# Long convolution with a gate: the large stores of a_u issued by GpSimd, positions in four loads, a sixth tile for x and v

## The chip, the cores and the metric

The kernel runs on one core of a Trainium2 chip. The metric is the time of one execution on the device in microseconds (us), lower is better: 1128.43 us as the median of three runs (1128.22 to 1131.92). The engines are named as in the profile: PE (matmuls), DVE and ACT (elementwise and copies), POOL (GpSimd), SP (which here only issues DMAs). DMAs can be issued by SP, ACT and POOL.

## What is computed

For x and v of shape (4, 12800, 128):

```
h = (relu(pos_emb @ w1) @ w2) * exp(-0.01 * t)        # a filter as long as the sequence
y = irfft(rfft(x * v) * rfft(h))[:12800]              # causal long convolution per channel
a = x * y
gate = sigmoid(sum_k conv_w[k] * shift(a, 4 - k))     # 5 taps
out = (gate * (a @ w_val)) @ w_out
```

Everything is float32. The transforms of length 25600 are done as matmuls with tables, split into 2 x 100 x 64 points.

## The kernel before

The work has three stages, each with its own tile pools. Stage 1 (lines 237 to 394) multiplies x by v, does the first short transform over 100 points, and writes the spectra to a DRAM scratch tensor `a_u` (52 MB). It also makes the filter's spectra. Stage 2 (lines 397 to 525) reads `a_u` back, does the 64-point transforms, multiplies by the filter and writes `c_y` to DRAM. Stage 3 reads `c_y`, finishes the inverse, gates and projects.

The change touches stage 1 alone. It is a loop over n = 0 to 63 (line 368), with its instructions in the order in which they are written (`manual_schedule`); each engine executes its own in that order. Step n does this:

- `fetch(n + 7)`: SP issues the load of 1 MB of x and v (line 311) into one of the `XB` = 5 tiles of `held`, used in turn.
- `product(n + 3)`: DVE multiplies x by v (line 317). An even one goes to a tile `u` of its own; an odd one goes back into the loaded tile, so that this tile is held until `mirrored` has read it.
- `mirrored(q + 1)`, every second step: DVE makes sums and differences of two products in one of two `eo` tiles (lines 325, 326).
- `spectra(q, s)`: PE does 12 matmuls into two PSUM tiles (line 338), and ACT copies each to the tile `st`, of which there are four (line 340).
- some pieces of `filt()`, paced by the count of steps: first 16 pieces that read the positions (line 257), then 32 that transform them (lines 275 to 278), then 25 with the twiddles `fk` (lines 286 to 300).
- `store(q, s, st)`: the 100 rows of `st`, 8 KB each, go to `a_u` as two DMAs. ACT issues rows 0 to 95 (768 KB), POOL rows 96 to 99 (32 KB), both on line 345.
- in the first steps POOL also issues the loads of the tables (line 388).

The positions come in 16 loads of 200 KB, issued by SP (line 250) between the fetches into one tile with room for five of them, the sixth of the `ld` pool; `load_pos` is called after each of the first pieces of `filt`, and a load waits until the matmuls that read its place are done.

Every DMA signals its landing on a semaphore. Those issued by SP and by ACT share eight, in the order of the program, and those issued by POOL have eight others. A DMA waits, on the queue of the engine that issues it, until the one before it on its semaphore has landed. In the middle of the loop fetches and stores alternate on the eight, so that a fetch waits for the fetch four before it; at the end, where no fetch is left, the eight no longer alternate, and the store of step 57 has the semaphore of the last fetch.

At n = 60 SP issues the first loads of stage 2 into the same `ld` pool (line 384), and after the loop the rest of them (line 394), which wait for the last stores (line 218). Stage 2 starts when they have landed.

Of the kernel before, what the change touches and what calls it, by code (L numbers as in the profile page):

```python
# [23 lines left out]
B, S, D, FO, KC = 4, 12800, 128, 64, 5  # L24
J, N1, N2 = 2, 100, 64
M = N1 * N2
KG = 8
# [52 lines left out]
def _raw(pool, tables, src, name):  # L80
    raw = pool.tile(list(src.shape), mybir.dt.int64, name=name)
    tables.append((raw, src))
    return raw
# [46 lines left out]
def tile_longconv_gate(  # L130
# [20 lines left out]
    nc = tc.nc  # L151
# [16 lines left out]
    w1bd = const.tile([128, 128], F32, name="w1bd")  # L168
# [18 lines left out]
    def load():  # L187
        return ld.tile([128, 2048], F32, name="ld")

    ag_pool = ctx.enter_context(tc.tile_pool(name="ag", bufs=1))  # L190
    ag = ag_pool.tile([128, N1, J, FO], F32, name="ag")
# [45 lines left out]
    with tc.tile_pool(name="p1", bufs=1) as p1, tc.tile_pool(name="ps1", bufs=1, space=PSUM) as ps1:  # L237
        g_sb = p1.tile([N1, J, FO, N2], F32, name="g_sb")

        GN, E, XB = 8, 4, 5  # L240
        held = [load() for _ in range(XB + 1)]
        PE1 = GN // 2 * N1
        pos_held = held.pop()[:, 0:2048 // PE1 * PE1].rearrange("p (i q a) -> p i q a", q=GN // 2, a=N1)
        parts, pos_ts = [(c0, j) for c0 in range(0, N2, GN) for j in range(J)], []

        def load_pos():
            if len(pos_ts) < len(parts):
                c0, j = parts[len(pos_ts)]
                t = pos_held[:, len(pos_ts) % (2048 // PE1)]
                nc.sync.dma_start(out=t.rearrange("p q a -> p (q a)"), in_=pos[j, c0 // GN])  # L250
                pos_ts.append(t)

        def filt():
            for i, (n0, j) in enumerate(parts):
                gp = ps1.tile([N1, GN, FO], F32, name="gp", bufs=2)
                for q in range(GN // 2):
                    nc.tensor.matmul(
                        out=gp[:, 2 * q:2 * q + 2].rearrange("a n e -> a (n e)"),
                        lhsT=pos_ts[i][:, q], rhs=w1bd, start=True, stop=True)
                nc.vector.scalar_tensor_tensor(  # L260
                    g_sb[:, j, :, n0:n0 + GN], gp.rearrange("a n e -> a e n"), 0.0,
                    win[:, j, n0:n0 + GN].unsqueeze(1).to_broadcast([N1, FO, GN]),
                    op0=ALU.max, op1=ALU.mult)
                load_pos()
                yield 1.5

            for j in range(J):
                for e0 in range(0, FO, E):
                    ap = ps1.tile([128, E, N1], F32, name="ap", bufs=2)
                    for e in range(E):  # L270
                        terms = [(j, 0, 1)] if j == 0 else [(1, 0, 1), (0, 1, 2)]
                        for i, (jj, wr, wi) in enumerate(terms):
                            lhs = g_sb[:, jj, e0 + e]
                            fl = dict(start=(i == 0), stop=(i == len(terms) - 1))
                            nc.tensor.matmul(out=ap[0:N2, e], lhsT=lhs, rhs=fwd[:, wr], **fl)
                            nc.tensor.matmul(out=ap[N2:2 * N2, e], lhsT=lhs, rhs=fwd[:, wi], **fl)
                    nc.scalar.copy(
                        out=ag[:, :, j, e0:e0 + E].rearrange("p k e -> p e k"), in_=ap)
                    yield 1.0 + 0.7 * j

            after = None
            for k0 in range(0, N1, 4):
                fk = p1.tile([128, 4, 2 * N2], F32, name="fk", bufs=2)
                for i in range(4):
                    k1 = k0 + i
                    nc.scalar.activation(fk[:, i], dft[:, 1], AF.Copy, scale=tw[:, 1, k1:k1 + 1])
                for i in range(4):
                    k1 = k0 + i
                    nc.vector.scalar_tensor_tensor(
                        fk[:, i], dft[:, 0], tw[:, 0, k1:k1 + 1], fk[:, i], op0=ALU.mult, op1=ALU.add)  # L290
                if after:
                    after()

                def after(k0=k0, fk=fk):
                    gz = ps1.tile([128, 4, 2 * N2], F32, name="gp", bufs=2)
                    for i in range(4):
                        nc.tensor.matmul(
                            out=gz[:, i], lhsT=ag[:, k0 + i].rearrange("p j e -> p (j e)"), rhs=fk[:, i],
                            start=True, stop=True)
                    nc.scalar.copy(out=ag[:, k0:k0 + 4].rearrange("p k j e -> p k (j e)"), in_=gz)  # L300
                yield 1.9
            after()
            yield 0.5
# [5 lines left out]
        def fetch(i):  # L309
            t = held[i % XB]  # L310
            nc.sync.dma_start(out=t, in_=xv[n_seq[i]].rearrange("h q w j l b d -> (h q) (w j l b d)"))
            fetched[i] = t.rearrange("p (w e) -> p w e", w=2)

        def product(i):
            t = fetched.pop(i)
            u = p1.tile([128, J * 2 * XE], F32, name="u", bufs=1) if i % 2 == 0 else t[:, 0]
            nc.vector.tensor_tensor(u, t[:, 0], t[:, 1], op=ALU.mult)
            us[i] = u

        def mirrored(q):  # L320

            a, b = us.pop(2 * q), us.pop(2 * q + 1)
            eo = held_e[q % 2]
            for s, op in ((0, ALU.add), (1, ALU.subtract)):
                nc.vector.tensor_tensor(eo[:, s].rearrange("p j l e -> p (j l e)"), a, b, op=op)  # L325
                nc.vector.tensor_tensor(eo[:, s, :, 0], eo[:, s, :, 0], eo[:, s, :, 1], op=ALU.subtract)
            eos[q] = eo
# [13 lines left out]
            return st  # L341

        def store(q, s, st):
            for eng, r in ((nc.scalar, slice(0, 96)), (nc.gpsimd, slice(96, N1))):
                eng.dma_start(  # L345
                    out=a_u[r, s, q].rearrange("k e j b d -> k (e j b d)"),
                    in_=st[r].rearrange("k e j b d -> k (e j b d)"))

        fetched, us, eos = {}, {}, {}
        with tc.manual_schedule():  # L350
            held_e = [p1.tile([128, 2, J, 2, XE], F32, name=f"eo{i}") for i in range(2)]
            fetch(0)
            raws = [
                (dst, _raw(p1, tables, src, f"raw{i}"))
                for i, (dst, src) in enumerate(((wval, w_val), (wout, w_out), (cw, conv_w.rearrange("k d -> d k"))))]
            fil = filt()
            narrow = (None for dst, raw in raws for _ in _narrow(nc, p1, dst, raw))
            n_fil, spent = 16 * 1.5 + 16 * 1.0 + 16 * 1.7 + 25 * 1.9 + 0.5, 0.0
            for i in range(1, XB):
                fetch(i)  # L360
                load_pos()
            product(0)
            product(1)
            mirrored(0)
            product(2)
            for i in (XB, XB + 1):
                fetch(i)
            for n in range(N2):
                q, s = divmod(n, 2)
                if n + XB + 2 < N2:  # L370
                    fetch(n + XB + 2)
                if n + 3 < N2:
                    product(n + 3)
                if s == 0 and q + 1 < N2 // 2:
                    mirrored(q + 1)
                st = spectra(q, s)
                while spent < n_fil * (n + 1) / (N2 - 6):
                    step = next(fil, None)
                    if step is None:
                        break  # L380
                    spent += step
                if n == N2 - 4:
                    for p in range(2):
                        loaded[p] = load_pair(p, NL)
                store(q, s, st)
                if n and tables:
                    dst, src = tables.pop(0)
                    nc.gpsimd.dma_start(out=dst, in_=src)
                if n >= 14:
                    next(narrow, None)  # L390
            for _ in fil:
                pass
            for p in range(2):
                load_a(loaded[p][0], p, NL, N2 // 2)


    with tc.tile_pool(name="p2", bufs=1) as p2, tc.tile_pool(name="psz", bufs=1, space=PSUM) as psz, \
# [62 lines left out]
        with tc.manual_schedule():  # L460
            for p in range(-1, NP + 1):
# [8 lines left out]
                if p == 41:  # L470
                    j, g = y_order[0]
                    nc.sync.dma_start(
                        out=xr_first, in_=xt[j][:, g * R:(g + 1) * R].rearrange("d n b a -> d (n b a)"))
# [23 lines left out]
                if now:  # L497
# [6 lines left out]
                    if old:  # L504
                        held = p2.tile([128, 1], F32, name="held", bufs=2)
# [30 lines left out]
    with tc.tile_pool(name="y3", bufs=1) as y3, tc.tile_pool(name="psy", bufs=1, space=PSUM) as psy, \  # L536
# [147 lines left out]
        with tc.manual_schedule():  # L684
# [7 lines left out]
            for i in range(R * NT + AHEAD3 + R + 3):  # L692
                (s, r), (t, rt) = divmod(i, R), divmod(i - AHEAD3, R)
                if r == 0 and s < NT:
                    if s + 1 < NT:
                        load_rows(s + 1)
                    j, g = y_order[s]
# [79 lines left out]
```

## Time and profile before

| | |
|---|---|
| median of 3 runs | 1128.43 us |
| profiled execution | 1130.9 us |
| its span, first to last instruction | 1128.9 us |
| stage 1, to the first matmul of stage 2 | 341 us |
| PE, DVE, ACT, POOL busy | 92%, 87%, 55%, 62% of the span |
| DMA, mean over the span | 317 GB/s |
| chain that ended last | PE 63%, DMA 22%, DVE 11%, ACT 3% |

The profile is of one execution. A share of the DMA near 1.0 in a stretch means that all 16 DMA engines had packets in work; the GB/s beside it say how fast those packets went. "Idle before" of an instruction is the time for which its engine had nothing to do, with what ended it behind the arrow. Times in the rows are microseconds from the start of the span.

### The profile page before, as it was taken

Reading aid. Unit: us, or ns where it says so; the run is one execution under the profiler, and the core shown is the slowest. Engines: PE = TensorE matmul, PEld = TensorE weight load, DVE = VectorE, ACT = ScalarE, POOL = GpSimd, SP = SyncE. Lnnn points to the kernel's source line nnn. Section 1 sums busy time; section 2 is a strip of 40 time slices with the busy share of each in tenths; the row PEclk is TensorE's granted clock in tenths of the full one; section 3 lists DMA queues with packets and bytes.
Section 4 is the critical chain, followed back from the end, with each engine's and each line's share of the span. In section 5 each row is a group of like instructions: output and inputs, shape, how many; then the busy total and the mean of one; then the engine's idle time right before and its main releaser. Section 6 shows DMA issues by size and latency. Waiting matters only on the chain.

```text
span 1128.9 us, 17155 instructions
## 1 busy us (share of the span) xinstructions
PE 1038.0 (92%) x6204; PEld 490.9 (43%) x6204; DVE 980.8 (87%) x1214; ACT 619.1 (55%) x1003; POOL 698.1 (62%) x405
## 2 busy tenths in 40 slices
PE   5789997977868999999999999979999999999996
PEld 2345654534423444444444444434444444444442
DVE  6677657888817999999999999739999999999997
ACT  1347665866642444444344444346767777767673
POOL 1111110100016888898898889638999899999981
PEclk9899999999986999999999999998999999999999
DMA  9999999999987788888988999566888888888842
GB/s 376 414 415 410 395 380 368 391 371 372 338 263 245 257 302 310 304 298 309 315 302 288 373 339 329 163 193 262 342 318 346 305 349 314 350 313 351 314 181 116
DMA packets 87771, 357.95 MB, mean 317 GB/s; under 512 B 9269, under 2 KB 18278, under 8 KB 65073
## 3 DMA queue, kind: packets, MB, share of 16 engines
q1 hardware_dynamic: 45768, 224.74, 55.0%
q10 hardware_dynamic: 39408, 129.18, 29.3%
q0 software_dynamic: 2512, 2.94, 0.9%
q8 instruction: 50, 0.82, 0.3%
q14 instruction: 33, 0.26, 0.1%
HBM read 225.76 MB, written 131.07 MB: 316 GB/s over the span
## 4 chain that ended last, share of the span: by engine, by line
PE 63%; DMA 22%; DVE 11%; ACT 3%; issue 1%; SPq 0%; ACTq 0%; DVEq 0%
PE c_ps L442 20%; DMA ld<-in_xv_dram 17%; PE sd L601 9%; PE z_ps L426 9%; PE o_ps L664 7%; PE v_ps L654 6%; PE tp L615 5%; PE fp L338 3%; DMA ld<-in_pos_dram 3%; PE c_ps L411 2%; DVE gt L643 2%; DVE eo L325 2%; DMA c_y<-c_sb 1%; DVE va L432 1%; DVE vb L432 1%
## 5 line engine op out<-in xcount | busy, mean ns | idle before, releaser
L628 POOL TENSOR_TENSOR ext<-yr,xr 128x400 f32<-128x400 f32 x120 | 304.4, 2538 | 38.1 <-DVE yr L626 32.7
L643 DVE SCALAR_TENSOR_TENSOR gt<-ext,cw,gt 128x1600 f32<-128x1600 f32 x128 | 242.7, 1896 | 2.4 <-ACT gt L640 2.4
L338 PE MATMUL fp<-eo,fold 64*128 64x512 f32 x768 | 194.8, 643 | 35.2 <-ACT st L340 19.0
L446 ACT COPY c_sb<-c_ps 128x1024 f32<-128x1024 f32 x100 | 101.3, 1013 | 207.3 <-PE c_ps L442 207.3
L345 POOL DMA_DIRECT2D a_u<-st x64 | 33.2, 519 | 290.4 <-ACT st L340 245.2
L340 ACT COPY st<-fp 128x1024 f32<-128x1024 f32 x128 | 126.7, 1016 | 117.9 <-PE fp L338 81.7
L442 PE MATMUL c_ps<-va,ld 64*128 64x512 f32 (+1 forms) x800 | 165.7, 554 | 0.0
L432 DVE TENSOR_TENSOR va<-z_ps,h_sb 128x2048 f32<-128x2048 f32 x50 | 114.5, 2290 | 30.4 <-PE z_ps L426 30.4
L426 PE MATMUL z_ps<-ld 64*64 64x512 f32 x800 | 123.0, 619 | 9.8 <-DMA ld<-a_u 8.7
L601 PE MATMUL sd<-ag,fold 100*64 100x512 f32 (+1 forms) x512 | 127.9, 617 | 2.9 <-DMA ag<-c_y 2.9
L509 POOL TENSOR_TENSOR va<-va,vb 128x1024 f32<-128x1024 f32 x49 | 116.0, 2367 | 15.9 <-DVE vb L432 15.9
L338 PEld LDWEIGHTS fp<-eo,fold 64*128 64x128 f32 x768 | 73.4, 199 | 115.4 <-issue 59.8
L442 PEld LDWEIGHTS c_ps<-va,ld 64*128 64x128 f32 x800 | 74.1, 189 | 112.2 <-issue 111.7
L664 PE MATMUL o_ps<-gd,wout 128*128 128x400 f32 x256 | 111.5, 517 | 10.7 <-DVE gd L659 9.8
L513 POOL TENSOR_TENSOR va<-va,vb 128x1024 f32<-128x1024 f32 x50 | 119.1, 2383 | 0.0
L432 DVE TENSOR_TENSOR vb<-z_ps,h_sb 128x2048 f32<-128x2048 f32 x50 | 114.0, 2281 | 0.0
L608 ACT COPY sd_sb<-sd 128x512 f32<-128x512 f32 x128 | 76.7, 599 | 57.6 <-PE sd L601 57.0
L654 PE MATMUL v_ps<-ext,wval 128*128 128x400 f32 x256 | 107.3, 501 | 0.0
L442 PE MATMUL c_ps<-vc,ld 64*128 64x512 f32 x400 | 94.2, 589 | 0.0
L615 PEld LDWEIGHTS tp<-ident,sd_sb 128*128 128x128 f32 x512 | 58.9, 142 | 79.2 <-PE sd L601 48.7
L510 POOL TENSOR_TENSOR vc<-vc,vd 128x768 f32<-128x768 f32 x49 | 89.2, 1820 | 1.9
L615 PE MATMUL tp<-ident,sd_sb 128*128 128x128 f32 x512 | 81.0, 283 | 4.7 <-ACT sd_sb L608 3.4
(86 smaller groups left out, 1484.9 us busy)
## 6 DMA issues: line engine op xcount, KB each, us to landing
ld<-in_xv_dram SPq DMA_DIRECT2D x64, 1024.0 KB
ag<-c_y SPq DMA_DIRECT2D x58, 1024.0 KB
c_y<-c_sb ACTq DMA_DIRECT2D x100, 512.0 KB
a_u<-st ACTq DMA_DIRECT2D x64, 768.0 KB
ld<-a_u SPq DMA_DIRECT2D x48, 1024.0 KB
xr<-in_xt_dram SPq DMA_DIRECT2D x31, 800.0 KB
out_dram<-o_sb ACTq DMA_DIRECT2D x31, 800.0 KB
ld<-in_tab_w_dram SPq DMA_DIRECT2D x12, 768.0 KB
```

Source lines behind the costliest of these rows:

```text
L338: nc.tensor.matmul(out=fp[:, h], lhsT=fold[r, w], rhs=eo[r, o, :, l], start=i == 0, stop=i == len(terms) - 1)
L340: nc.scalar.copy(out=st[:, o].rearrange("k j (h b) d -> k h j (b d)", h=2), in_=fp)
L426: nc.tensor.matmul(out=zs[c][half[h]], lhsT=wk[half[c], 0, half[h]], rhs=a2[half[c], h, j], start=True, stop=True)
L432: nc.vector.tensor_tensor(out, z.rearrange("p (b d) -> p b d", d=D).unsqueeze(1).to_broadcast([128, n, B, D]), h_sb.unsqueeze(2).to_broadc ...
L442: nc.tensor.matmul(out=c_ps[:, h, 0:n], lhsT=wk[half[h], 1 + c], rhs=vt[half[h]].rearrange("p b d -> p (b d)"), start=(i == 0), stop=(i == ...
L513: nc.gpsimd.tensor_tensor(va[:, 2:4], va[:, 2:4], vb[:, 2:4], op=ALU.add)
L601: nc.tensor.matmul(out=sd[c * N2:(c + 1) * N2], lhsT=inv[k, s // NG, c], rhs=ct[c][k, r * B * D:(r + 1) * B * D], start=True, stop=True)
L615: nc.tensor.transpose(out=tp[:, b], in_=t[:, b], identity=ident)
L628: nc.gpsimd.tensor_tensor(e[:, r0 + r], yr, xr, op=ALU.mult)
L643: nc.vector.scalar_tensor_tensor(gt, rows(t, k), cw[:, k:k + 1], gt, op0=ALU.mult, op1=ALU.add)
L654: nc.tensor.matmul(out=v_ps, lhsT=wval, rhs=rows(t)[:, r * ROW:(r + 1) * ROW], start=True, stop=True)
L664: nc.tensor.matmul(out=o_ps, lhsT=wout, rhs=gd, start=True, stop=True)
```

## The change

Three things change in stage 1. POOL issues both DMAs of a store. The positions are laid out on the host so that four loads of 800 KB bring all of them, to the tile `ag`, which later takes the filter's spectra; they are issued once, behind fetches 1 to 4. And the tile that held positions is now a sixth one for x and v (`XB` = 6), so that the fetch in step n is number n + 8.

```
-        GN, E, XB = 8, 4, 5
-        held = [load() for _ in range(XB + 1)]
+        GN, E, XB = 8, 4, 6
+        held = [load() for _ in range(XB)]
...
+        pos_ts = ag.rearrange("p k j e -> p (k j e)")[:, 0:len(parts) * PE1].rearrange(
+            "p (i q a) -> p i q a", q=GN // 2, a=N1)
+
+        def load_pos(i):
+            nc.sync.dma_start(out=pos_ts[:, 4 * i:4 * i + 4].rearrange("p i q a -> p (i q a)"), in_=pos[i])
...
-                        lhsT=pos_ts[i][:, q], rhs=w1bd, start=True, stop=True)
+                        lhsT=pos_ts[:, i, q], rhs=w1bd, start=True, stop=True)
...
-                load_pos()
                 yield 1.5
...
         def store(q, s, st):
-            for eng, r in ((nc.scalar, slice(0, 96)), (nc.gpsimd, slice(96, N1))):
-                eng.dma_start(
+            for r in (slice(0, 96), slice(96, N1)):
+                nc.gpsimd.dma_start(
...
             for i in range(1, XB):
                 fetch(i)
-                load_pos()
+                if i < 5:
+                    load_pos(i - 1)
```

## Rows read from the trace of the kernel before

**Rows 1.** The page, part 2: the span in 40 slices of 28 us.
```profile
DMA  9999999999987788888988999566888888888842
GB/s 376 414 415 410 395 380 368 391 371 372 338 263 245 257 302 310 304 298 309 315 302 288 373 339 329 163 193 262 342 318 346 305 349 314 350 313 351 314 181 116
```
**Rows 2.** Stretches: length, busy us (instructions) of PE, PEld, DVE, ACT, POOL, clock, DMA, GB/s.
```profile
56.00:85.00 29.00, 25.91 (x162) 13.76 (x158) 22.77 (x25) 14.35 (x15) 5.11 (x9) 1.00 1.02 415
...
113.00:285.00 172.00, 148.76 (x1108) 83.90 (x1108) 129.96 (x209) 115.55 (x190) 17.64 (x34) 0.96 0.99 380
285.00:311.00 26.00, 21.27 (x108) 10.84 (x104) 22.42 (x34) 16.63 (x31) 2.59 (x5) 1.00 0.97 330
311.00:338.00 27.00, 17.96 (x92) 7.34 (x92) 5.06 (x5) 11.85 (x12) 3.11 (x6) 0.84 0.84 270
```
**Rows 3.** SP's waits from 64 to 345 us: in total, times, longest.
```profile
SPq L311 <- DMA ld<-in_xv_dram: 153.5, 36, 8.1
SPq L311 <- DVE eo L325: 42.7, 11, 8.6
```
**Rows 4.** ACT in order of time from 268 to 346 us: start, duration, idle before.
```profile
299.82 0.31 ACTq L345 DMA_DIRECT2D a_u<-st  x1
...
304.17 0.58 ACT L300 COPY ag<-gp 128x512 f32<-128x512 f32 x1 [0.62 <-PE gp L297]
311.35 0.31 ACTq L345 DMA_DIRECT2D a_u<-st  x1
311.78 1.93 ACT L340 COPY st<-fp 128x1024 f32<-128x1024 f32 x2 [7.03 <-DMA ld<-in_xv_dram]
...
331.30 0.31 ACTq L345 DMA_DIRECT2D a_u<-st  x1
```
**Rows 5.** DVE in order of time from 284 to 346 us.
```profile
311.30 1.23 DVE L317 TENSOR_TENSOR ld<-ld 128x1024 f32<-128x1024 f32 x1 [0.39 <-DMA ld<-in_xv_dram]
314.97 1.23 DVE L325 TENSOR_TENSOR eo<-u,ld 128x1024 f32<-128x1024 f32 x1 [2.45 <-PE fp L338]
316.24 0.69 DVE L326 TENSOR_TENSOR eo<-eo 128x512 f32<-128x512 f32 x1
```
**Rows 6.** PE in order of time, at 124 us and from 310 us.
```profile
124.48 2.85 PE L338 MATMUL fp<-eo,fold 64*128 64x512 f32 x12
128.78 1.56 PE L338 MATMUL fp<-eo,fold 64*128 64x512 f32 x6
...
312.85 8.48 PE L338 MATMUL fp<-eo,fold 64*128 64x512 f32 x24 [5.94 <-ACT st L340]
```
**Rows 7.** The chain that ended last, at the end of stage 1: start, duration.
```profile
296.46 14.81 DMA ld<-in_xv_dram
...
331.30 6.66 DMA a_u<-st
```
**Rows 8.** DMAs that POOL issues: ns least, median, most; the last row is landing.
```profile
L345 POOL DMA_DIRECT2D a_u<-st x64: 517/518/534, 19.3 to 331.6; - x64
...
DMA to landing us min/median/max: 4.8/6.7/9.2
...
L388 POOL DMA_DIRECT2D dft<-in_tab_dft_dram x1: 598/598/598, 39.6 to 39.6; - x1
```
**Rows 9.** DMA queues from 113 to 198 us: packets, MB, share of 16 engines.
```profile
q1 hardware_dynamic: 2492, 18.16, 56.4%
q10 hardware_dynamic: 1939, 13.58, 40.3%
q0 software_dynamic: 545, 0.56, 2.0%
```
**Rows 10.** SP's loads of positions: ns least, median, most, first and last start.
```profile
L250 SPq DMA_DIRECT2D ld<-in_pos_dram x16: 327/355/465, 1.7 to 61.6; - x16
```
**Rows 11.** Odd products of DVE, the first and the last of six from 113 to 169 us.
```profile
114.56 1.22 DVE L317 TENSOR_TENSOR ld<-ld 128x1024 f32<-128x1024 f32 x1 [2.60 <-DMA ld<-in_xv_dram]
...
168.20 1.23 DVE L317 TENSOR_TENSOR ld<-ld 128x1024 f32<-128x1024 f32 x1 [3.60 <-DMA ld<-in_xv_dram]
```

More of the change, by code (lines that the diff above doesn't have):

```diff
@@ L238, in tile_longconv_gate @@
         g_sb = p1.tile([N1, J, FO, N2], F32, name="g_sb")
-        GN, E, XB = 8, 4, 5
-        held = [load() for _ in range(XB + 1)]
+        GN, E, XB = 8, 4, 6
+        held = [load() for _ in range(XB)]
         PE1 = GN // 2 * N1
[L243 to L251, printed above, removed]
+        parts = [(c0, j) for c0 in range(0, N2, GN) for j in range(J)]
+        pos_ts = ag.rearrange("p k j e -> p (k j e)")[:, 0:len(parts) * PE1].rearrange(
+            "p (i q a) -> p i q a", q=GN // 2, a=N1)
+        def load_pos(i):
+            nc.sync.dma_start(out=pos_ts[:, 4 * i:4 * i + 4].rearrange("p i q a -> p (i q a)"), in_=pos[i])
         def filt():
@@ L758 @@
     pos = np.asarray(inputs["pos_emb"]).reshape(J, N1, N2 // KG, KG // 2, 2, FO)
-    pos = np.transpose(pos, (0, 2, 4, 5, 3, 1)).reshape(J, N2 // KG, 2 * FO, KG // 2 * N1)
+    pos = np.transpose(pos, (2, 0, 4, 5, 3, 1)).reshape(4, 4, 2 * FO, KG // 2 * N1)
+    pos = np.transpose(pos, (0, 2, 1, 3)).reshape(4, 2 * FO, 2 * KG * N1)
     feeds[:0] = [("xv", xv), ("xt", xt), ("pos", pos)]
```

## The prediction, made before the changed kernel was run

> **What bounds the kernel now.** I read the page's slices first, then stage 1 by stretches, then the waits of the engine that issues the loads, then the end of the stage in order of time. The slices show where to look: the DMA is full for the first eleven slices, some 310 us, and falls in the twelfth [rows 1]. That is stage 1, the only one whose code changes; stages 2 and 3 should keep their length and start when it ends. So the question is what stage 1 loses.
>
> The stretches split it in three [rows 2]. From 56 to 85 us the share is 1.02 at 415 GB/s. From 113 to 285 us it is 0.99 at 380 GB/s, from 285 to 311 us 0.97 at 330 GB/s, and from 311 to 338 us 0.84 at 270 GB/s. So the loop runs at the pace of its transfers: a step moves a load of 1,048,576 bytes and a store of 819,200, and DVE's odd product waits for a landed load each time [rows 11]. Between the two rows shown there are ten steps in 53.64 us, 5.4 us each, while PE's own round in the same place, from the start of one step's matmuls to the next, is 4.30 us [rows 6]. Compute has room, the DMA little.
>
> The waits of SP say what holds the loads: 153.5 us, in 36 waits, until an earlier load has landed, and 42.7 us until DVE has freed a tile [rows 3]. The first is the shared semaphores: only four fetches can be under way.
>
> The end of the stage is another matter. ACT copies at 304.17 us and then nothing until 311.35, where it issues a store; the copy behind it shows 7.03 us of idle time ended by a load of x and v [rows 4]. The store needed only ACT's own copies. It waited because its semaphore was that of the last fetch, and every later copy waited behind it. The last fetch lands as DVE's last product starts, 311.30 us [rows 5]. From there the last store is issued 20.0 us later, at 331.30 [rows 4], lands 6.66 us after [rows 7], and stage 2 waits for that. PE shows why it takes 20: at 312.85 it begins the steps that had piled up, the first 24 matmuls (two steps) in 8.48 us [rows 6], where two steps of the middle take 2 x 2.85 = 5.70: the granted clock of the stretch is 0.84, against 0.96 and 1.00 before [rows 2], so partly 1.2 instead of 2.4 GHz.
>
> **The change part by part.**
>
> *The stall of ACT goes.* With the stores on POOL, ACT waits for no load. What is late next is the last load itself. From its landing at 311.30 the chain is product 1.23, sums 1.23, correction 0.69 [rows 5], two steps of matmuls 2 x 2.85 [rows 6], and a last copy of 0.97 (half of the 1.93 for two, rows 4): 9.8 us, and some 0.3 between instructions. Before it was 20.0, so 9.9 less. If PE ran both steps at the speed of its 8.48 us for two, the chain is 2.8 longer, and if three steps are piled up another 2.9: 4.2 less. I take 9.9, bounds 4.2 and 10.2 (nothing between instructions).
>
> *The withheld stores compete.* Before, ACT issued no store between 299.82 and 311.35 [rows 4], and the last loads had the DMA to themselves. In the changed kernel four more stores (steps 57 to 60) come ahead of the last landing: 4 x 819,200 bytes at 380 GB/s [rows 2] are 8.6 us. Against it, the sixth tile lets SP issue the last fetch about a step sooner: it was issued at 296.46 [rows 7], and a step is 4.9 us (POOL's stores run from 19.3 to 331.6, rows 8: 63 steps in 312.3). Net 3.7 us later, bounds 0 and 8.6.
>
> *The fetches.* With loads alone on the eight semaphores, a fetch waits for the one eight before it, which six tiles never reach; the 153.5 us of waiting turn into waits for a tile or vanish. They are worth only what the DMA idles: 0.03 of 172 us and 0.05 of 26 us against the share of 1.02 [rows 2], 5.2 + 1.3 = 6.5 us. The slower packets (380 against 415 GB/s at nearly the same share) are not a matter of the queue's depth as far as the rows show. I take 2.0 of it, since the waits for a tile stay; bounds 0 and 6.5.
>
> *POOL's issues.* 64 more DMAs of 96 rows. The trace has no such one; POOL needs 0.518 us for 4 rows of 8 KB and 0.598 for 128 rows of 1 KB [rows 8], so some 0.6 us, 64 x 0.6 = 38 us on an engine that is busy 17.64 of 172 us in the middle [rows 2]. A step then costs POOL 1.1 us of 4.9. Behind a waiting store stand only its twin, the next stores, and the tables, in the first eleven steps; PE needs the first table only when the 16 position pieces are done. Cost 0, and ACT loses 64 issues of 0.31 us that nobody waited for.
>
> *Packets of the software queue.* They could be slower than ACT's. From 113 to 198 us ACT's queue used 40.3% of 16 engines for 13.58 MB, 548 us of engine time or 0.33 us per 8 KB; POOL's used 2.0% for 0.56 MB, 27 us for 68 such rows (17 stores of four) with all its small packets counted in, at most 0.40 us each [rows 9]. If all of the difference held, 64 x 96 / 16 x 0.07 = 27 us. But POOL's queue had 477 packets besides the 68 rows, and 10 ns for each of these would explain all of it: 0. They are tiny (0.56 MB is the rows alone), so I take 0; the 27 us are in the rivals.
>
> The Trainium skill's page "SBUF — State Buffer" (section "SBUF: two separate sides") warns of this very move: a DMA issued from GpSimd has its descriptors written by GpSimd, and a DVE operation in a two-port mode locks it out meanwhile; it advises issuing from ACT or SP. By that rule the two issues of the last store would each wait for a DVE instruction of up to 1.23 us, 2.5 us in all, and the sum would be -5.7. The trace does not agree for the operations used here: with DVE busy 130 of 172 us [rows 2], POOL's 64 issues took 517 to 534 ns [rows 8].
>
> *Landing.* POOL's 32 KB stores land 4.8 to 9.2 us after issue [rows 8], ACT's last one in 6.66 [rows 7]. A copy into `st` waits for the store four steps back, 4 x 4.9 = 19.6 us, less about 3 us for the copies themselves: it binds only beyond 16.6 us. Cost 0; at the last store from -2 to +2.5, the same two numbers against 6.66.
>
> *Positions.* All bytes are as before, 3.28 MB, but 4 x 614,400 of them move ahead of fetches 2 to 5: 6 us of the DMA at 415 GB/s, which delays the first steps by up to that and is given back up to 61.6 us, when the old loads ended [rows 10]. The cover is a full DMA; if steps 2 to 5 could not catch up it costs 6 us. Compute's 4.30 against the 4.9 of a step says that they can: 0. The waits of SP for the positions' place go, and no fetch stands behind them.
>
> Sum: -9.9 + 3.7 - 2.0 = -8.2 us, on the profiled execution 1130.9 - 8.2 = 1122.7. That execution lay 2.5 us over the median of 1128.43; from the median it is 1120.2, my forecast. All bounds together (with 2 less and 2.5 more for landing, 6 more for the positions) give -18.7 to +12.9: 1110 to 1141 without the 27 us.
>
> **The rivals.**
>
> *The transfers give nothing back (no change).* The DMA is the bound, and what ACT no longer loses the last loads do. For it: shares of 0.97 to 1.02 until 311 us [rows 2]. Against it: 0.84 in the last 27 us. The tail gives its lower bound of 4.2, the competing stores take 3.7, nothing else: -0.5, 1127.9. The Trainium skill's "DMA: Bandwidth & Descriptors" (section "Issuing engines are not separate DMA queues") says as much: the issuing engine saves only the time of issuing, the 16 engines are the same. By that rule the gain would be near 0; the trace agrees on the full DMA and shows at 311 us a wait that the rule does not cover.
>
> *Slower: POOL's queue is the slower one.* One mechanism, the price of a row of 8 KB in the software queue. At 0.40 us against 0.33 [rows 9] the stage grows by 27 us, less 8.2: 1147. It decides from 0.33 + 8.2 x 16 / 6144 = 0.35 us on. For it: 0.40 as the outer bound; against it, the small packets that are counted in.
>
> *Much faster.* If the four-deep queue of loads is why packets slow down after 113 us, they go at 415 again: 172 x 380 + 26 x 330 = 73.9 MB in 178 us instead of 198, 20 less, and with the tail's -9.9 + 3.7 it is 1102. Against it: nothing in the shares (0.99 and 0.97) says that engines lacked work.
>
> **How the numbers follow.** Forecast 0.54 (own range 1114 to 1126), no change 0.25, slower 0.12, much faster 0.09. A run of this kernel can tell about 0.5% from no change, 5.6 us: faster is below 1122.8, slower above 1134.1. Of the forecast 0.8 lies below 1122.8, of "no change" a quarter: faster 0.43 + 0.06 + 0.09 = 0.58; same 0.11 + 0.19 = 0.30; slower 0.12. The range 1108 to 1132 leaves out most of the slower case and half of the much faster.
>
> **What would show it.** Right: no idle time of ACT ended by a load; the last store within 10 to 13 us of the last product; the first matmul of stage 2 near 333 us instead of 341; SP waiting for DVE rather than for loads. POOL's 96-row issues near 0.6 us, its queue's engine time per MB that of ACT's before. Wrong: shares under 0.95 in the middle, copies into `st` waiting for a landed store, or the last product some 9 us later than 311.30.

## The result: 1112.91 us, 1.5% faster

The changed kernel takes 1112.91 us (median of four runs, 1110.98 to 1113.54) against 1129.05 of the kernel before beside it (1128.22 to 1131.92). The ratio is 0.9849, with an interval of 0.9817 to 0.988. That is 7.3 us under the forecast of 1120.2, below its own range of 1114 to 1126 and inside the whole range.

In the profiles the first matmul of stage 2 starts at 323.33 us instead of 341.17, 17.8 us earlier; the rest of the kernel has its old length. Line numbers are three lower than before: L308 is the fetch, L314 the product, L337 the copy into `st`, L342 the store.

The page's slices of the changed kernel, of 27.8 us each, answer to [rows 1]: its rates hold at 422 to 425 GB/s until the seventh slice.

```profile
DMA  9999999999985888888889998568888888888842
GB/s 378 417 418 425 423 424 422 405 401 389 329 277 208 307 293 315 291 295 301 309 297 340 370 325 281 168 179 324 317 347 316 329 336 327 332 329 335 325 169 118
```

The stretches of the changed kernel, with the columns of [rows 2]:

```profile
56.00:85.00 29.00, 26.48 (x198) 14.42 (x196) 24.62 (x27) 14.62 (x16) 8.31 (x15) 1.00 1.01 419
113.00:285.00 172.00, 154.36 (x1128) 84.02 (x1125) 137.44 (x226) 121.64 (x209) 36.92 (x72) 0.99 1.00 405
285.00:311.00 26.00, 21.89 (x100) 9.18 (x99) 16.77 (x20) 16.17 (x22) 7.17 (x14) 1.00 0.96 334
311.00:338.00 27.00, 13.74 (x104) 5.24 (x104) 12.49 (x10) 5.10 (x13) 8.34 (x7) 0.66 0.79 264
```

In the middle the share of the DMA is what it was, 1.00 after 0.99, and the rate is 405 GB/s instead of 380: the engines had no more time in work, they moved more in it. In 172 us that is 4.3 MB more, 11 us at the new rate.

SP's waits in the changed kernel from 64 to 345 us, against [rows 3]:

```profile
SPq L308 <- DVE eo L322: 124.7, 23, 9.3
SPq L308 <- DVE u L314: 34.5, 15, 3.6
SPq L218 <- DMA a_u<-st: 33.8, 5, 15.1
SPq L308 <- DMA ld<-in_xv_dram: 26.2, 13, 2.6
```

The 153.5 us of waiting for a landed load have become 26.2; SP now waits for DVE to free a tile. ACT's longest group of waits in the same stretch:

```profile
ACT st L337 <- DMA a_u<-st: 49.8, 32, 2.5
```

ACT waits for no load any more, but 32 times for a store that still holds a tile `st`. In the kernel before, its waits for loads in the same stretch were these, five in all and not the one at the end alone:

```profile
ACT st L340 <- DMA ld<-in_xv_dram: 19.2, 5, 7.0
```

The second longest of them lies in the middle of the loop. There ACT copies nothing until it has issued a store at 188.24 us, and that store waits for a load, while DVE goes on with products at 183.30 and 185.59:

```profile
188.67 1.93 ACT L340 COPY st<-fp 128x1024 f32<-128x1024 f32 x2 [6.14 <-DMA ld<-in_xv_dram]
```

So the alternation of fetches and stores on the eight semaphores breaks here too, and not only at the end of the loop: this store is on the semaphore of the load issued at 172.86.

The end of the stage in order of time, first DVE's last product (it answers to the first line of [rows 5]), then POOL's last stores and ACT's copies:

```profile
297.05 1.22 DVE L314 TENSOR_TENSOR ld<-ld 128x1024 f32<-128x1024 f32 x1
```

```profile
297.51 1.02 POOL L342 DMA_DIRECT2D a_u<-st  x2 [6.43 <-ACT st L337]
298.72 1.02 POOL L342 DMA_DIRECT2D a_u<-st  x2 [0.19 <-issue]
301.31 1.02 POOL L342 DMA_DIRECT2D a_u<-st  x2 [1.56 <-ACT st L337]
304.41 1.02 POOL L342 DMA_DIRECT2D a_u<-st  x2 [2.07 <-ACT st L337]
308.51 1.02 POOL L342 DMA_DIRECT2D a_u<-st  x2 [3.08 <-ACT st L337]
311.94 1.02 POOL L342 DMA_DIRECT2D a_u<-st  x2 [2.40 <-ACT st L337]
```

```profile
306.29 1.93 ACT L337 COPY st<-fp 128x1024 f32<-128x1024 f32 x2 [2.17 <-DMA a_u<-st]
309.72 1.93 ACT L337 COPY st<-fp 128x1024 f32<-128x1024 f32 x2 [1.50 <-DMA a_u<-st]
```

The chain that ended last, there: it runs through landed stores and the copies into `st` that waited for them, up to the last store and stage 2's first load.

```profile
299.23 10.39 DMA a_u<-st
309.64 0.04 ACTq L337
309.68 0.04 issue
309.72 1.94 ACT st L337 x2
311.65 0.28 issue
311.94 8.44 DMA a_u<-st
320.39 2.90 DMA ld<-a_u
323.29 0.04 issue
323.33 2.09 PE z_ps L424 x8
```

POOL's issues on the line of the stores, against [rows 8]: the 96-row ones, half of them, cost no more than the 4-row ones, and their landing takes 15.2 us.

```profile
L342 POOL DMA_DIRECT2D a_u<-st x128: 515/518/551, 19.7 to 312.4; - x128
```

The queues from 113 to 198 us, against [rows 9]: 43.5% of 16 engines in 85 us are 592 us for 15.39 MB, 0.315 us per 8 KB with the small packets counted in; ACT's queue had 0.33. SP's queue, the loads, went from 0.346 us per 8 KB to 0.313.

```profile
q1 hardware_dynamic: 2800, 20.38, 57.2%
q0 software_dynamic: 2716, 15.39, 43.5%
```

### The profile page after: what moved, and what is told of

Its sections match the earlier page's. It is cut to its first block, busy times and chain, and to the rows that moved or that the text cites. A ratio compares the mean times of both kernels' runs of the same rounds, so it can differ in the third digit from the quotient of the medians.

```text
span 1110.8 us, 17154 instructions
## 1 busy us (share of the span) xinstructions
PE 1031.7 (93%) x6204; PEld 483.9 (44%) x6204; DVE 980.8 (88%) x1214; ACT 616.1 (55%) x1003; POOL 730.8 (66%) x469
## 4 chain that ended last, share of the span: by engine, by line
PE 65%; DMA 22%; DVE 6%; ACT 5%; issue 1%; POOL 1%; ACTq 0%; SPq 0%; DVEq 0%; POOLq 0%
PE c_ps L440 21%; DMA a_u<-st 18%; PE sd L599 11%; PE z_ps L424 9%; PE o_ps L662 7%; PE v_ps L652 6%; PE tp L613 5%; PE fp L335 3%; DMA ld<-in_xv_dram 3%; PE c_ps L409 2%; ACT st L337 2%; DVE gt L641 1%; DVE va L430 1%; DVE vb L430 1%; POOL a_u L342 1%
## 5 line engine op out<-in xcount | busy, mean ns | idle before, releaser
L335 PE MATMUL fp<-eo,fold 64*128 64x512 f32 x768 | 188.7, 625 | 31.7 <-ACT st L337 18.4
L342 POOL DMA_DIRECT2D a_u<-st x128 | 65.8, 518 | 231.1 <-ACT st L337 133.1
L337 ACT COPY st<-fp 128x1024 f32<-128x1024 f32 x128 | 124.3, 1015 | 118.2 <-DMA a_u<-st 49.8
L335 PEld LDWEIGHTS fp<-eo,fold 64*128 64x128 f32 x768 | 69.4, 192 | 111.5 <-issue 50.7
## 6 DMA issues: line engine op xcount, KB each, us to landing
a_u<-st POOLq DMA_DIRECT2D x64, 768.0 KB, 15.2
```

What stands on the lines that cost most here:

```text
L335: nc.tensor.matmul(out=fp[:, h], lhsT=fold[r, w], rhs=eo[r, o, :, l], start=i == 0, stop=i == len(terms) - 1)
L337: nc.scalar.copy(out=st[:, o].rearrange("k j (h b) d -> k h j (b d)", h=2), in_=fp)
```

## The experiments

Ratios are to the kernel before, with their intervals. "Middle" is 113 to 285 us, "end" 285 to 311 us, in GB/s.

### Which part it is

`e1_act_stores` is the changed kernel with the 96-row stores back on ACT:

```
-            for r in (slice(0, 96), slice(96, N1)):
-                nc.gpsimd.dma_start(
+            for eng, r in ((nc.scalar, slice(0, 96)), (nc.gpsimd, slice(96, N1))):
+                eng.dma_start(
```

> The changed kernel with one part undone: ACT issues the 96-row stores again; the four position loads and the six tiles stay. Theory A (the eight shared semaphores were the limit: with ACT's stores on them only four fetches can be under way, and the store at the end waits for the last fetch): no gain over the kernel before, 0.995 to 1.005 of it, 1125 to 1134 us, ACT again idle some 7 us at the end until a load of x and v, and 113 to 285 us at about 380 GB/s. Theory B (the sixth tile is what brings the transfers back to 420 GB/s): about half of the gain stays, 8 us, 1121 us.

Measured: 1125.7 us, 0.9957 (0.9925 to 0.9989). Middle 384, end 352. ACT is again idle at the end, 9.55 us, here until a load for stage 2 (`ld<-in_tab_w_dram`) has landed. SP waits 173.0 us for landed loads, more than before, though it has six tiles:

```profile
SPq L308 <- DMA ld<-in_xv_dram: 173.0, 38, 7.0
```

`e2_five_tiles` is the changed kernel with the sixth tile unused:

```
-        GN, E, XB = 8, 4, 6
-        held = [load() for _ in range(XB)]
+        GN, E, XB = 8, 4, 5
+        held = [load() for _ in range(6)]
```

> The changed kernel with five tiles for x and v instead of six (the sixth stands unused); POOL issues all stores, positions in four loads. Theory A: most of the gain stays, 10 to 16 of the 16 us, 1113 to 1119 us, because five fetches may now be under way where four could before, and ACT waits for no load. Theory B: only the end of the stage is better, some 6 to 8 us, 1121 to 1123 us, and 113 to 285 us stays at 380 GB/s.

Measured: 1116.78 us, 0.9859 (0.9814 to 0.9905); middle 402. The sixth tile is worth 3.9 us by the medians, within the intervals of both: that it is worth anything is not shown.

`e3_stores_only` is the kernel before with nothing but `store` changed:

```
-            for eng, r in ((nc.scalar, slice(0, 96)), (nc.gpsimd, slice(96, N1))):
-                eng.dma_start(
+            for r in (slice(0, 96), slice(96, N1)):
+                nc.gpsimd.dma_start(
```

> The kernel before with one part of the change: POOL issues the 96-row stores; sixteen position loads and five tiles as before. Theory A: as with five tiles and four position loads, within 2 us (1113 to 1121 us), since only the stores matter. Theory B: 1121 to 1124 us. If the positions matter (theory C: SP stands behind the waits of the 16 position loads), it is 3 us or more slower than the kernel with five tiles and four position loads.

Measured: 1115.86 us, 0.9862 (0.9814 to 0.9909); middle 401, end 359. SP's wait for loads is already down to 38.0 us:

```profile
SPq L311 <- DVE eo L325: 115.9, 23, 9.6
SPq L311 <- DMA ld<-in_xv_dram: 38.0, 22, 4.1
```

`e4_positions_only` is the kernel before with the four loads of positions into `ag`, five tiles, stores on ACT (cut to the calls):

```
+        def load_pos(i):
+            nc.sync.dma_start(out=pos_ts[:, 4 * i:4 * i + 4].rearrange("p i q a -> p (i q a)"), in_=pos[i])
...
-                load_pos()
+                if i < 5:
+                    load_pos(i - 1)
```

> The kernel before with one part of the change: positions in four loads to the place of the spectra; ACT issues the 96-row stores, five tiles (the sixth unused). Theories A and B: no change, 1126 to 1132 us. Theory C: 3 to 6 us faster.

Measured: 1127.9 us, 0.9985 (0.9956 to 1.0014); middle 381. The positions are worth nothing that can be measured.

What follows: the stores alone give a ratio of 0.9862, where the whole change gives 0.9849; they carry the gain. Without them the other two parts bring 0.4%.

### The tiles `st`, and the loads under way

`e5_st5` gives the changed kernel a fifth `st` (the tile `u` moves to `xr_first`), `e6_four_tiles` four load tiles (`XB` = 4, the same four loads of positions, issued behind the first fetches; their lines are left out):

```
-            u = p1.tile([128, J * 2 * XE], F32, name="u", bufs=1) if i % 2 == 0 else t[:, 0]
+            u = xr_first[:, 0:J * 2 * XE] if i % 2 == 0 else t[:, 0]
...
-            st = p1.tile([128, 2, J, B, D], F32, name="st", bufs=4)
+            st = p1.tile([128, 2, J, B, D], F32, name="st", bufs=5)
```

```
-        GN, E, XB = 8, 4, 6
+        GN, E, XB = 8, 4, 4
```

> The changed kernel with a fifth tile st (the even products go to the tile that later takes the first rows of x in stage 2, which makes room). In the changed kernel ACT's copies wait 49.8 us in all for a landed store, and the chain that ended last in stage 1 is mostly stores. Theory D (the four st tiles are now the bound): those waits vanish and the stage ends 5 to 10 us earlier, 1103 to 1108 us. Theory E (the DMA is full at about 424 GB/s up to 198 us, so a fifth tile only lengthens the queue): the stores land later, about 20 us after issue instead of 15, and the time is the same within 3 us, 1110 to 1116 us.

> The changed kernel with four tiles for x and v (two stand unused); POOL issues all stores. Theory A1 (the rate from 113 to 198 us, 382 GB/s before and 422 now, is a matter of how many loads are under way; with four tiles at most four, fewer than before): the rate falls back to 380 to 390 GB/s and the time to 1122 to 1132 us. Theories A2 (the queue that carries the stores) and A3 (stores that ACT no longer holds up): 410 to 424 GB/s, 1115 to 1121 us.

`e5_st5`: 1115.6 us, 0.9853 (0.9818 to 0.9887). The stores land later, 17.8 us instead of 15.2, and ACT waits for them no less than in the changed kernel (57.5 us for 49.8): a further tile takes nothing off these waits and nothing off the time, as theory E has it. `e6_four_tiles`: 1114.83 us, 0.985 (0.9822 to 0.9878). From 113 to 198 us it moves 395 GB/s, between the numbers of the theories; its time is that of A2 and A3. The middle is 390, the end 369. The rate in the middle falls with the tiles, the time hardly does: of what it loses there it has a part back by 311 us.

```profile
113.00:285.00 172.00, 153.03 (x1124) 83.59 (x1120) 132.87 (x217) 120.17 (x206) 36.60 (x73) 0.99 0.99 390
285.00:311.00 26.00, 21.67 (x101) 9.54 (x100) 19.73 (x26) 15.99 (x23) 7.02 (x14) 1.00 1.00 369
```

### The end of the stage alone

`e7_last_stores` is the kernel before with the stores from step 56 on issued by POOL:

```
+            big = nc.gpsimd if 2 * q + s >= 56 else nc.scalar
+            for eng, r in ((big, slice(0, 96)), (nc.gpsimd, slice(96, N1))):
```

> The kernel before, only that POOL issues the 96-row stores from step 56 on. It takes away the stall of ACT behind the last fetch and nothing else. By the prediction's first two terms the stage ends 9.9 - 8.6 to 9.9 us earlier, 1 to 10, most likely 6: 1124 us, 0.994 of before; the rate from 113 to 285 us stays at 380 GB/s. If the stall is worth nothing by itself (the stores lengthen the last loads by as much): within 2 us of before.

Measured: 1128.19 us, 0.9988 (0.9959 to 1.0017). In its profile, of an execution of 1123.93 us, the last store is issued at 323.19 instead of 331.30 and stage 2 starts 6.7 us earlier, where the prediction's two terms for the end have 6.2 (-9.9 + 3.7). That the sums agree is chance, for the terms don't: the last product is 1.6 us earlier and not 3.7 later, from there to the last store it is 13.5 us, 6.5 less and not 9.9, and from the last store to stage 2 1.4 more. The executions spread from 1122.42 to 1135.17, and the profiled one is among the fastest; in the medians at most 4.6 us of the gain (0.9959) can be there. ACT still waits 3.89 us for a load at step 55's store, and 6.28 us at 188.87. The earlier stores, which `e3_stores_only` has on top of this, are worth 12.3 us between the two medians (14 by the two ratios, since the runs were made beside different runs of the kernel before).

### The two queues exchanged

`e8_loads_pool` lets POOL issue the loads of x and v and ACT all stores; the tables go to SP. `e9_loads_pool_tables_pool` is the same with the tables left on POOL (without the last two lines).

```
-            nc.sync.dma_start(out=t, in_=xv[n_seq[i]].rearrange("h q w j l b d -> (h q) (w j l b d)"))
+            nc.gpsimd.dma_start(out=t, in_=xv[n_seq[i]].rearrange("h q w j l b d -> (h q) (w j l b d)"))
...
-                nc.gpsimd.dma_start(
+                nc.scalar.dma_start(
...
-                    nc.gpsimd.dma_start(out=dst, in_=src)
+                    nc.sync.dma_start(out=dst, in_=src)
```

> The changed kernel with the queues the other way round: POOL issues the loads of x and v, ACT both DMAs of a store, SP the positions and the tables; six tiles. Loads and stores again share no semaphores, but the stores are in the queue that they had before. Theories A1 and A3: 410 to 424 GB/s from 113 to 198 us as in the changed kernel, 1111 to 1117 us. Theory A2 (stores in ACT's hardware queue are what slows the packets): 380 to 390 GB/s, 1120 to 1130 us.

> The changed kernel with the two queues exchanged: POOL issues the loads of x and v (and the tables), ACT issues both DMAs of every store. The stores have the eight hardware semaphores to themselves, the loads have POOL's eight. Theory A (loads and stores on the same semaphores and hardware queues slow each other): the middle, 113 to 198 us, moves about 420 GB/s as in the changed kernel (422), and the time is 1111 to 1117 us. Theory A2 (a store issued by ACT is slow by itself): 385 GB/s as with ACT's stores and SP's loads, and 1122 us or more. If the rate is 420 but the time stays above 1122, the start of the stage pays: tables issued by POOL behind its loads, or loads that POOL issues late; 56 to 85 us then stays under 400 GB/s.

`e8_loads_pool`: 1129.28 us, 0.9966 (0.9938 to 0.9995). From 113 to 198 us it moves 422 GB/s, as the changed kernel does, so a store issued by ACT is not slow as such. It loses its time at the start, where ACT's stores share semaphores with SP's tables: from 56 to 85 us it moves 264 GB/s. ACT's longest wait from 20 to 113 us:

```profile
ACT st L337 <- DMA raw<-in_moe_conv_w_dram: 16.3, 1, 16.3
```

`e9_loads_pool_tables_pool`: 1126.73 us, 0.9966 (0.9944 to 0.9989). Neither theory had its numbers: the rate from 113 to 198 us is 399, between their two. The start is whole (415 GB/s from 56 to 85 us), but the stall is back at the end: ACT's last stores now share semaphores with SP's first loads of stage 2, and ACT stands still behind them. ACT in order of time:

```profile
302.58 1.93 ACT L337 COPY st<-fp 128x1024 f32<-128x1024 f32 x2 [4.79 <-DMA ld<-a_u]
312.08 0.69 ACTq L342 DMA_DIRECT2D a_u<-st  x2
312.81 1.93 ACT L337 COPY st<-fp 128x1024 f32<-128x1024 f32 x2 [8.31 <-DMA ld<-a_u]
```

All kernels in which ACT waits for some load before it issues a store took 1125 us or more (the kernel before and `e1_act_stores`, `e4_positions_only`, `e7_last_stores`, `e8_loads_pool`, `e9_loads_pool_tables_pool`); all without such a wait took 1113 to 1117. The rate in the middle doesn't sort them: `e8_loads_pool` moves 422 GB/s from 113 to 198 us and takes 1129.28 us, `e6_four_tiles` moves 395 and takes 1114.83. And from step 16 to step 32, by the start of the second copy of each into `st`, the kernel before takes 74.4 us and the changed one 73.6, though from 113 to 181 us, which lies for the most part in these steps, they move 385 and 424 GB/s.

The wait of 6 us in the middle of the loop is part of this. It stands at about 188 us in all four kernels with loads on SP and stores on ACT (the kernel before, `e1_act_stores`, `e4_positions_only`, `e7_last_stores`: 6.0 to 6.5 us). From step 32 to step 36 these four take 23.4 to 24.4 us; the five with POOL's stores take 17.7 to 19.9. `e8_loads_pool` takes 18.4, and `e9_loads_pool_tables_pool` 24.8 with no wait of ACT for a load there, which stays open.

### The transfers by themselves

Three kernels of DMAs alone. `d1_copy_act` and `d2_copy_pool` differ in one word, the engine of the 96-row stores:

```
    for n in range(N2 + 4):
        if n < N2:
            nc.sync.dma_start(out=held[n % 10], in_=xv[n_seq[n]]...)
        if n >= 4:
            for eng, r in ((nc.scalar, slice(0, 96)), (nc.gpsimd, slice(96, N1))):   # d2: nc.gpsimd twice
                eng.dma_start(out=a_u[r, s, q]..., in_=held[(n - 4) % 10][r])
```

> Only DMAs: all computation and stages 2 and 3 are left out. SP issues 64 loads of 1 MB into ten tiles, and each landed tile is stored to a_u, 96 rows by ACT and 4 rows by POOL. So loads and stores have the two hardware queues and the eight semaphores they had before the change, but no engine paces them. If two hardware queues side by side (or the shared semaphores) are what slows the packets, this moves about 380 GB/s and lasts some 310 us (64 x 1.87 MB = 119.5 MB); if the kernel's pacing is the cause, about 420 GB/s and 285 us.

> As the kernel of DMAs alone with ACT's stores, but POOL issues the 96-row stores too, on its own queue and semaphores. If the queues are the cause, about 420 GB/s and 285 us, against 380 GB/s and 310 us with ACT; if pacing is, both kernels are alike. If the software queue is the slower one for rows of 8 KB when nothing else runs, this is the longer of the two.

Measured: 325.19 us with ACT's stores and 309.19 with POOL's, one run each (310 and 285 were expected); from 56 to 285 us 382 and 411 GB/s, and from 95 to 240 us 377 and 426. So a difference in rate like that of the middle is there with no compute at all, and 16 us with it: pacing by the engines is not needed for it.

`d3_queues` (one run) asks which property of the queues it is: seven parts over the same places in memory.

```
    phases = [   # loads, 96-row stores, 4-row stores, a small load after each; the loop is left out
        ((nc.sync, nc.sync), nc.scalar, nc.gpsimd, False),
        ((nc.sync, nc.sync), nc.gpsimd, nc.gpsimd, False),
        ((nc.sync, nc.sync), nc.gpsimd, nc.gpsimd, True),
        ((nc.sync, nc.sync), nc.sync, nc.gpsimd, False),
        (sp_act, nc.gpsimd, nc.gpsimd, False),
        ((nc.gpsimd, nc.gpsimd), nc.scalar, nc.scalar, False),
        ((nc.sync, nc.sync), nc.scalar, nc.gpsimd, False),
    ]
```

> Only DMAs again, all computation and stages 2 and 3 left out: seven parts of 32 steps each, all over the same 32 MB of x and v and the same places of a_u, one part after the other, 59.8 MB each. 1: loads by SP, 96-row stores by ACT (as before the change). 2: loads by SP, stores by POOL (as changed). 3: as 2, with a load of 512 bytes by SP after each, so that a load waits for the load four before it, as in 1. 4: loads and 96-row stores by SP, one hardware queue. 5: loads by SP and ACT in turn, stores by POOL. 6: loads by POOL, all stores by ACT. 7: as 1. If loads on one hardware queue and stores on the other are what makes packets slow: 1 and 7 about 380 GB/s, the rest about 425. If it is the wait for the load four before, or the shared semaphores: 1, 3, 4 and 7 about 380. If it is that ACT's queue stores: 1, 6 and 7 about 380. If it comes with the place in memory or the time since the start: all parts alike, or 7 other than 1.

A stretch inside each part, in order: length, POOL's busy time, clock, share, GB/s.

```profile
20.00:140.00 120.00, 12.44 (x24) 1.00 1.00 402
190.00:270.00 80.00, 17.93 (x36) 1.00 1.01 426
290.00:420.00 130.00, 25.64 (x50) 1.00 0.96 344
460.00:580.00 120.00, 15.21 (x30) 1.00 1.01 398
620.00:740.00 120.00, 23.19 (x45) 1.00 0.98 378
...
800.00:905.00 105.00, 11.08 (x21) 1.00 1.01 427
940.00:1060.00 120.00, 12.89 (x25) 1.00 0.99 384
```

The large loads issued in the same stretches (parts 1 to 4, 6 and 7): their count, and the median us from issue to landing.

```profile
held<-in_xv_dram SPq DMA_DIRECT2D x23, 1024.0 KB, 24.1
...
held<-in_xv_dram SPq DMA_DIRECT2D x18, 1024.0 KB, 34.4
...
held<-in_xv_dram SPq DMA_DIRECT2D x23, 1024.0 KB, 20.5
...
held<-in_xv_dram SPq DMA_DIRECT2D x25, 1024.0 KB, 18.9
...
held<-in_xv_dram POOLq DMA_DIRECT2D x21, 1024.0 KB, 33.6
...
held<-in_xv_dram SPq DMA_DIRECT2D x24, 1024.0 KB, 19.9
```

Count times landing over the length of the stretch gives the loads under way: 4.6, 7.7, 3.6, 3.9, 6.7 and 4.0. The two parts with 6.7 and 7.7 move 426 and 427 GB/s, one with POOL's queue storing, one with it loading; the others have five or fewer and 344 to 402. Part 3 against part 2 has the same queues, with a load of 512 bytes after each step and by it the wait for the load four before, and 82 GB/s less. Not all of that is the wait: parts 1 and 7 have it too, without small loads, and move 402 and 384. Part 4 against parts 1 and 7: one hardware queue instead of two, 398 against 402 and 384. So two hardware queues side by side are not what makes packets slow, and neither is the place in memory. In these transfers the slow parts are those with five loads under way or fewer, and in parts 1, 3, 4 and 7 it is the wait for the load four before that holds the number down. Part 5 was to be at 425 by the first three theories and is at 378. SP's loads in it landed after 12.3 us, so that of the 26 in 120 us fewer than three were under way; what held them back was not tested by itself.

## Why the prediction came out as it did

The sign and the part of the code were right: the stores leave the semaphores of the loads, and the gain is stage 1's. The sum was too small by half. The end, from which the prediction had 9.9 us, gave 3.6, and what comes before the last product, which it had at 1.7 us lost, gave 14.25; that the time still fell inside the whole range is in part luck. In the two profiles:

| | predicted | measured |
|---|---|---|
| last product (311.30 before) | +3.7 - 2.0 | 297.05, -14.25 |
| from there to the last store (20.0 before) | -9.9 | 311.94 - 297.05 = 14.9, -5.1 |
| from there to the first matmul of stage 2 (341.17 - 331.30 = 9.9 before) | 0 | 323.33 - 311.94 = 11.4, +1.5 |
| sum | -8.2 | -17.8 |

*The fetches* (-2.0, bounds 0 and 6.5) are the term that was furthest off. It priced the 153.5 us of waiting only by the DMA's idle share, and set the slower packets aside as "not a matter of the queue's depth as far as the rows show". The share indeed stayed, 0.99 and 1.00; the rate rose from 380 to 405. A full share therefore was no bound on the gain: an engine whose packet takes longer counts as busy too (0.346 and 0.313 us per 8 KB in SP's queue). `e3_stores_only` less `e7_last_stores`, 12.3 us, is what the stores before step 56 are worth in time. It is not the price of the slower packets alone, for a second thing is in it, which the prediction had at nothing.

*ACT's waits for loads ahead of the end* are that second thing. The prediction saw the stall of 7.03 us; the kernel before has 19.2 us of such waits from 64 us on, 6.14 of them at 188.67, where four steps take some 4 to 6 us longer than in the kernels with POOL's stores. The two are not separated: that store waits for a load, and slower packets make the load late. `e6_four_tiles` and `e8_loads_pool` speak for the waits as the larger part; against it, `d1_copy_act` loses as much as the whole gain to `d2_copy_pool` with no compute to hold up.

*The much faster rival* (0.09) named a queue of four loads as the cause of the slow packets. `d3_queues` bears it out for the transfers by themselves. Its size was too large: it had 415 GB/s until 311 us, where 405 and 334 came. And in the full kernel depth alone doesn't explain the time: `e6_four_tiles` has four tiles, 390 GB/s in the middle, and all of the gain.

*The stall of ACT goes*: right, no idle time of ACT is ended by a load. The tail behind the last product got 5.1 us shorter and not 9.9, and is 14.9 us where the prediction's sign was 10 to 13: the sum counted the matmuls of two steps, and PE had four left (297.01 to 310.26 us), ahead of the last of the six stores shown; the copies of the last two wait 2.17 and 1.50 us for a tile `st`. "It binds only beyond 16.6 us" missed the end: landings of 8 to 15 us bind there, because there the copies follow each other every 3 to 4 us and not once a step of 4.9. That a copy into `st` waits was named as a sign against the forecast; it came, and `e5_st5` shows that a fifth tile gains nothing by it.

*The withheld stores compete* (+3.7): not seen as a loss. The stretch from 285 to 311 us kept its rate, 334 after 330, and the last product came earlier, not later. In `e7_last_stores` too the last product came earlier, by 1.6 us.

*POOL's issues* were taken at 0.6 us and took 0.52; nothing in the chain waits for them. The Trainium skill's "SBUF — State Buffer", section "SBUF: two separate sides", warned of DVE, in a two-port mode, locking out POOL's descriptor writing. With DVE busy 137 of 172 us the 128 issues took 515 to 551 ns: no such wait is seen in them, and no run shows whether DVE's operations here use that mode. *Packets of the software queue*: 0, and 0; 0.315 us per 8 KB is below the 0.33 of ACT's queue, which ends the slower rival. *Positions*: 0, and 0.9985.

*No change* (0.25) rested on the DMA being full. The Trainium skill's "DMA: Bandwidth & Descriptors", section "Issuing engines are not separate DMA queues", says that the issuing engine changes only the time of issuing. Part 4 of `d3_queues` agrees, as far as the queue itself goes: one hardware queue moves as much as two (398 against 402 and 384 GB/s). But moving the stores changed which semaphores they wait on, and with that came 14 us of the kernel (`e3_stores_only`); the rule doesn't cover this.

What stays open: why packets take longer when few loads are under way, and why `e6_four_tiles` and `e8_loads_pool` (POOL's loads land in 17.9 us there, 36 in 172 us, so 3.7 under way, at 406 GB/s) don't follow the rule that the transfers by themselves show. How much of the 14 us is ACT's waiting for loads and how much the slower packets is open too. No run had ACT's stores and no semaphore shared with a load at all.

## What to carry to other kernels

A full DMA share is not a ceiling: look at the GB/s beside it, and if it falls while the share stays, ask how many transfers are under way and what keeps that number down. Where loads and stores take turns on a set of shared semaphores, a load waits for the load a fixed number before it; and wherever the alternation breaks, at the ends of the loop or once within it, a store can wait for an unrelated load, and all that its engine has to do waits behind it. List such waits of the engine over the whole loop, not only where the page points. Taking the stores off the set of the loads of x and v and of the next stage was worth 1.4% here (`e3_stores_only`), another buffer nothing that could be told from noise.

## What was not expected of the hardware

- The same transfers moved 378 to 427 GB/s by nothing but who issued them and what they waited for, at shares of 0.98 to 1.01; with a load of 512 bytes after each step, 344 at 0.96.
- POOL's issue of a DMA of 96 rows of 8 KB takes as long as one of 4 rows, both 0.52 us; of 128 rows of 8 KB 0.53 (`e9_loads_pool_tables_pool`).
- Kernels whose stores ACT issues spread by 6 to 13 us over 8 to 10 runs (`e1_act_stores` 1121 to 1134), those whose stores POOL issues by 1 to 4 us over four.
